# Attention outputs turned in 32x32 blocks by VectorE, four heads stacked, with the projection's weights padded to four chunks of 128

## The chip, the cores and the metric

The kernel runs on one core of a Trainium2 chip. The metric is the device time of one execution in microseconds, given as the median of several runs. Times inside the program come from one profiled execution on the same kind of chip.

## The reference

One transformer block is computed: 2048 tokens, width 448, 16 heads of 28, a causal sliding window of 256 keys, a feed-forward part of width 1792 with Mish. Both halves are modulated by a conditioning vector.

```python
mod = (silu(c) @ w_mod).reshape(1, 6, 1, -1)
sa, ca, ga, sb, cb, gb = mod[:, 0], ..., mod[:, 5]
h = layernorm(x) * (1 + ca) + sa
q, k, v = split(h @ wqkv)                      # 16 heads of 28
p = softmax(mask(q @ k.T * 28 ** -0.5))        # 0 <= query - key < 256
x = x + ga * ((p @ v).concat_heads @ wo)
h = layernorm(x) * (1 + cb) + sb
x = x + gb * (mish(h @ w1 + b1) @ w2)
```

## The kernel before

The tokens are worked off in four groups of 512. Almost every product is made of two or three matmuls on the high and low parts of its operands (names with h and l: `hh`, `hl`, `Ph`, `Pl`, `wo3`, `wol`), so that float32 accuracy is kept.

**Heads.** There are 64 head steps s (4 groups of 16 heads), each of three units u = 3s + k, with k from 0 to 2. `A(i, t)` makes the scores of head i, queries t*128 onward, in a PSUM bank `sA` (two banks), and VectorE reduces them at once to a row maximum (`junk`, `mx`, L680, with an accumulator read). `M2(pr)` lets TensorE transpose the maxima of two heads (L686), VectorE splits them in two rows `mr`, and a DMA puts them beside q, so that `B(u)` computes scores less the maximum in `sB`. ScalarE takes the exponential twice (`P`, `Ph`), GpSimd subtracts to get `Pl` (`SP`, L730), and `PV` multiplies both with v into a bank `pv`: rows 0 to 27 and 28 hold the high part and the sum of weights, rows 32 to 59 the low part. A head's scores are made three heads ahead of their use.

**Outputs.** `EV` (L746; the last three heads on VectorE, L748) copies the 60 rows of `pv` to one of two tiles `O2`, two heads above each other. `E` (L754) lets TensorE transpose such a pair in four pieces into a bank `tr`; `E2` (ScalarE) copies the low part, `E3` takes the reciprocal of the sum, adds, and GpSimd multiplies into `on[g]`, tokens in the partitions. When all 16 heads of a group are there (`on_full`), `gen_oT` turns `on[g]` back with 16 TensorE transposes (`ot`, through `tr_chunk`, L249), ScalarE makes `hho`, VectorE `hlo`, and `gen_wo` multiplies with the output projection: three chunks of 128 features with three matmuls each, and a fourth of 64 with its two halves stacked, 11 matmuls for 128 tokens. Its result is added to x, stored to `x1d`, and its layer norm statistics taken.

**Order.** It is written out by hand: the loop at the end emits, for each unit u, the attention steps, and between them pieces of a filler (`fill_main`: query, key and value products, `gen_oT`, `gen_wo`, then layer norm and `gen_hT` of the next group) as long as a credit of `RATE[g]` lasts; each yield of the filler costs some of it. `fill_side` adds weight preparation, `pipe` delays the steps that empty a bank by a unit or two, and `later` holds DMA issues for the SP queue. Every engine works its own instructions in that order. `gen_hT` transposes the normed x into a bank, ScalarE makes `hh` (L256), VectorE scales the bank in place (`hT_y`, L253) and subtracts (L261).

**PSUM.** Eight banks: two `sA`, two `sB`, two `mm`, one `pv`, one `tr`, of which M2's and E's transposes share the last. After the heads the banks are given to the feed-forward: two `z`, four `acc`, two `tr`.

**Feed-forward.** For each n, 11 matmuls make `z` (L915), ScalarE Mish and `ah`, VectorE `al`, and 12 matmuls go to `acc` (L1098 to L1100). In the first 14 of them the weights are still split (`pieces`: ScalarE, then GpSimd), and a filler works off the projection of group 3, `gen_oT(3)` and `gen_wo(3)`, a few steps for each n.

Of the kernel before, what the change touches and what calls it, by code (L numbers as in the profile page):

```python
# [15 lines left out]
NG, GT = 4, 512  # L16
# [35 lines left out]
def adaln_block(ctx: ExitStack, tc: tile.TileContext, x, wqkv, wo, w1, b1, w2, c, w_mod, out):  # L52
# [104 lines left out]
    mask = kq.tile([128, 384], F32, name="mask")  # L157
# [100 lines left out]
    def hT_lo(p, ci, hh, hl, si, y=True):  # L258
        if y:
            hT_y(p, ci, si)  # L260
        DVE.tensor_tensor(hl[:, ci], p, hh[:, ci].bitcast(F32), op=ALU.subtract)  # L261
# [49 lines left out]
    def tile_mms(p, ps):  # L311
        m = 0
        for n, (a, b) in enumerate(ps):
            PE.matmul(p, b, a, start=(n == 0), stop=(n == 10))  # L314
            m += 1
            if m >= chunk["v"] and n < 10:
                yield cost(m, p.shape[-1])
                m = 0
# [181 lines left out]
    first_tiles([(0, bank("pv", 1, "qk0_0")), (3, bank("tr", 1, "qk0_3"))])  # L500
# [17 lines left out]
    O2 = []  # L518
    for i in range(2):
        t = att.tile([128, GT], F32, name=f"o2_{i}")  # L520
        POOL.memset(t[32:64, :], 0.0)
        O2.append(t)
    wo3 = [mid.tile([128, D], F32R, name=f"wo3_{i}", tag="wo", bufs=7) for i in range(4)]
    wol = [mid.tile([128, D], F32R, name=f"wol_{i}", tag="wo", bufs=7) for i in range(3)]
# [5 lines left out]
    def stg(pl, name):  # L530
        return pl.tile([128, 512], F32, name=name, tag="stg", bufs=4)
# [19 lines left out]
    def gen_mod_wo():  # L551
# [6 lines left out]
        pieces = []  # L558
        for ci in range(4):
            t = stg(qk, f"wop{ci}")  # L560
            pieces.append(t[:, 0:D])
            later.append(lambda ci=ci, t=t: load_piece(wo, ci, 0, D, t))
# [3 lines left out]
        for ci in range(4):  # L566
# [5 lines left out]
            split_lo(w, wo3[ci], wol[min(ci, 2)], ci, DVE)  # L572
# [40 lines left out]
    def gen_oT(g, tag, bufs, oT_pool):  # L613
        o = on[g]
        oh, ol = OT[g] = new_T(f"o{g}", oT_pool)

        def oT_out(p, ci):
            DVE.tensor_tensor(ol[:, ci], p, oh[:, ci].bitcast(F32), op=ALU.subtract)

        for ci in range(4):  # L620
            p = bank(tag, bufs, f"ot{g}{ci}")
            tr_chunk([o[:, t] for t in range(4)], ci, p)
            ACT.activation(oh[:, ci], p, AF.Copy)
# [12 lines left out]
    def gen_wo(g, tag, bufs):  # L636
# [14 lines left out]
        for t in range(4):  # L651
# [7 lines left out]
            for ci in range(3):  # L659
                ps += [(oh[:, ci, ts], wo3[ci]), (oh[:, ci, ts], wol[ci]), (ol[:, ci, ts], wo3[ci])]  # L660
            ps += [(oh[:, 3, ts], wo3[3]), (ol[:, 3, ts], wo3[3])]
# [6 lines left out]
    mx, Pt, Ph, Pl, pvb, et, olt = {}, {}, {}, {}, {}, {}, {}  # L668
    junk = att.tile([128, 384], F32, name="junk")

    def A(i, t):
# [5 lines left out]
        p = bank("sA", 2, f"sA{i}_{t}")  # L677
# [6 lines left out]
    def M2(pr):  # L684
        p = bank("tr", 1, f"mt{pr}")
# [57 lines left out]
    def EV(i):  # L743
        o = O2[i // 2 % 2][64 * (i % 2):64 * (i % 2) + 60]
        if i < NS - 3:
            ACT.activation(o, pvb[i][0:60, :], AF.Copy)  # L746
        else:
            DVE.tensor_copy(o, pvb[i][0:60, :])  # L748

    def E(pr):  # L750
        g, h = divmod(2 * pr, H)
        p = bank("tr", 1, f"et{pr}")
        for t in range(4):
            PE.transpose(p[:, t * 128:t * 128 + 124], O2[pr % 2][0:124, t * 128:(t + 1) * 128], ident[0:124, 0:124])  # L754
        et[pr] = p.rearrange("p (t a d) -> p t a d", t=4, a=2)

    def E2(pr):
        olt[pr] = att.tile([128, 4, 2, 28], F32, name=f"ol{pr}", tag="ol", bufs=2)
        ACT.activation(olt[pr], et[pr][:, :, :, 32:60], AF.Copy)

    def E3(pr):
        g, h = divmod(2 * pr, H)
        e, ol = et[pr], olt[pr]
        if h == 0:
            on[g] = mid.tile([128, 4, 512], F32, name=f"on{g}", tag="on")
        rc = att.tile([128, 4, 2, 1], F32, name=f"rc{pr}", tag="rc", bufs=2)
        DVE.reciprocal(rc, e[:, :, :, 28:29])
        DVE.tensor_tensor(ol, ol, e[:, :, :, 0:28], op=ALU.add)
# [411 lines left out]
```

## Time and profile before

| | |
|---|---|
| median of 3 runs | 717.61 us (717.17 to 718.66) |
| profiled execution, and its span | 719.96 us, 718.2 us |
| granted TensorE clock, mean | 0.99 |
| HBM read, written | 53.45 MB, 29.36 MB |
| attention, groups 1 and 2 | 139 to 241 and 241 to 343 us |
| feed-forward alone | from about 415 us |

In the profile PE is TensorE's matmuls, PEld its weight loads, DVE VectorE, ACT ScalarE, POOL GpSimd, SP the queue that issues the transfers. A row of a group names the source line, engine and operation, the tiles it writes and reads, the shape, the count, then busy us and mean ns, and the idle time just before with what ended it. A row of the timeline is start, duration, engine, line, tiles and count. A row of a table by windows gives for each engine the busy time and instructions, in the order PE, PEld, DVE, ACT, POOL, then the granted clock, the DMA share and GB/s.

### The profile page before, as it was taken

Reading aid. Unit: us, or ns where it says so; the run is one execution under the profiler, and the core shown is the slowest. Engines: PE = TensorE matmul, PEld = TensorE weight load, DVE = VectorE, ACT = ScalarE, POOL = GpSimd, SP = SyncE. Lnnn points to the kernel's source line nnn. Section 1 sums busy time; section 2 is a strip of 40 time slices with the busy share of each in tenths; the row PEclk is TensorE's granted clock in tenths of the full one; section 3 lists DMA queues with packets and bytes.
Section 4 is the critical chain, followed back from the end, with each engine's and each line's share of the span. In section 5 each row is a group of like instructions: output and inputs, shape, how many; then the busy total and the mean of one; then the engine's idle time right before and its main releaser. Section 6 shows DMA issues by size and latency. Waiting matters only on the chain.

```text
span 718.2 us, 12057 instructions
## 1 busy us (share of the span) xinstructions
PE 694.9 (97%) x4049; PEld 597.3 (83%) x4049; DVE 380.0 (53%) x1018; ACT 390.9 (54%) x740; POOL 327.0 (46%) x358
## 2 busy tenths in 40 slices
PE   8999999999999999999999899999999999999996
PEld 8777878788898888898887688888888888888885
DVE  5688657788555878656768642434323232322112
ACT  4538778768766768767868774243224222422221
POOL 6636778676666767666869744422010000000002
PEclk9999999999999999999999899999999999999999
DMA  7865763453761653744672165400200020001001
GB/s 215 257 211 178 251 204 122 148 158 125 212 207 50 203 166 88 230 137 137 216 223 75 52 216 157 116 1 2 102 1 1 4 99 1 0 7 45 0 1 51
DMA packets 48249, 83.86 MB, mean 117 GB/s; under 512 B 6142, under 2 KB 26348, under 8 KB 48188
## 3 DMA queue, kind: packets, MB, share of 16 engines
q1 hardware_dynamic: 47724, 83.10, 37.1%
q8 instruction: 32, 0.52, 0.3%
q14 instruction: 29, 0.24, 0.1%
q10 hardware_dynamic: 464, 0.00, 0.0%
HBM read 53.45 MB, written 29.36 MB: 115 GB/s over the span
## 4 chain that ended last, share of the span: by engine, by line
PE 72%; issue 11%; DVE 8%; DMA 4%; ACT 2%; POOL 1%; SPq 1%; POOLq 0%; DVEq 0%; ACTq 0%
PE z L915 15%; PE pv L740 9%; PE qk L314 8%; PE sA L678 5%; PE acc L1098 5%; PE acc L1100 5%; PE acc L1099 5%; PE sB L708 5%; PE wo L314 4%; PE qk_v L314 4%; PE sB L719 3%; DVE junk L680 3%; PE et L754 2%; DMA q<-mr 1%; DMA scr<-st 1%
## 5 line engine op out<-in xcount | busy, mean ns | idle before, releaser
L730 POOL TENSOR_TENSOR Pl<-P,Ph 128x512 fp32r<-128x512 f32 (+2 forms) x192 | 234.5, 1229 | 87.1 <-ACT Ph L723 49.4
L680 DVE CUSTOM_DVE_ANT_0 junk<-sA,mask 128x384 f32<-128x384 f32 (+2 forms) x256 | 135.2, 528 | 97.8 <-PE sA L678 89.5
L722 ACT ACTIVATE P<-sB 128x512 f32<-128x512 f32 (+2 forms) x192 | 109.8, 572 | 66.9 <-PE sB L719 61.7
L923 DVE TENSOR_TENSOR al<-t,ah 128x512 fp32r<-128x512 f32 x56 | 38.7, 692 | 199.7 <-ACT ah L922 199.7
L921 ACT ACTIVATE t<-z,b1c 128x512 f32<-128x512 f32 x56 | 38.5, 688 | 188.8 <-PE z L915 181.6
L723 ACT ACTIVATE Ph<-sB 128x512 fp32r<-128x512 f32 (+2 forms) x192 | 109.2, 569 | 0.0
L678 PE MATMUL sA<-k,q 84*128 84x384 f32 (+2 forms) x256 | 100.9, 396 | 2.2 <-DVE mx L680 1.5
L915 PE MATMUL z<-hhf,w 128*128 128x512 f32 x224 | 89.6, 400 | 0.0
L915 PE MATMUL z<-hlf,w 128*128 128x512 f32 x224 | 88.4, 395 | 0.0
L1098 PE MATMUL acc<-w2h,ah 128*128 128x448 f32 x224 | 82.0, 366 | 0.0
L1100 PE MATMUL acc<-w2h,al 128*128 128x448 f32 x224 | 81.7, 365 | 0.0
L1099 PE MATMUL acc<-w2l,ah 128*128 128x448 f32 x224 | 81.4, 364 | 0.0
L740 PE MATMUL pv<-Ph,v 128*60 128x256 f32 (+2 forms) x352 | 77.6, 295 | 3.6 <-DVE o L748 2.3
L740 PE MATMUL pv<-Pl,v 128*60 128x256 f32 (+2 forms) x352 | 74.4, 286 | 2.3 <-POOL Pl L730 2.3
L708 PE MATMUL sB<-q,k 86*128 86x256 f32 (+1 forms) x352 | 74.7, 286 | 1.4 <-DMA q<-mr 1.4
L915 PE MATMUL z<-hhf,w1l 128*128 128x512 f32 x168 | 66.3, 395 | 0.0
L708 PEld LDWEIGHTS sB<-q,k 86*128 86x128 f32 x352 | 62.4, 191 | 2.9 <-issue 1.2
L740 PEld LDWEIGHTS pv<-Ph,v 128*60 128x60 f32 x352 | 46.0, 135 | 18.0 <-ACT o L746 3.2
L719 PE MATMUL sB<-fdmask,identr 128*128 128x128 bf16 (+1 forms) x320 | 60.6, 255 | 0.0
L678 PEld LDWEIGHTS sA<-k,q 84*128 84x128 f32 x256 | 48.9, 192 | 8.5 <-DVE mx L680 5.9
L740 PEld LDWEIGHTS pv<-Pl,v 128*60 128x60 f32 x352 | 45.7, 133 | 11.0 <-POOL Pl L730 3.9
L1107 POOL TENSOR_TENSOR yo<-yo,x 128x448 f32<-128x448 f32 (+1 forms) x4 | 4.2, 1064 | 108.1 <-DVE yo L1104 108.1
(156 smaller groups left out, 1300.4 us busy)
## 6 DMA issues: line engine op xcount, KB each, us to landing
scr<-st SPq DMA_DIRECT2D x24, 512.0 KB
k<-scr SPq DMA_DIRECT2D x48, 252.0 KB
q<-scr SPq DMA_DIRECT2D x64, 168.0 KB
scr<-st SPq DMA_DIRECT2D x32, 256.0 KB
x<-x1d SPq DMA_DIRECT2D x10, 448.0 KB
xin<-in_A_x_dram SPq DMA_DIRECT2D x8, 448.0 KB
xr<-in_A_x_dram SPq DMA_DIRECT2D x16, 224.0 KB
x1d<-xr SPq DMA_DIRECT2D x16, 224.0 KB
```

The source lines that it names most:

```text
L314: PE.matmul(p, b, a, start=(n == 0), stop=(n == 10))
L678: PE.matmul(p[:, c0:384], q[0:84, t * 128:(t + 1) * 128], k[0:84, t * 128 + c0:t * 128 + 384], start=True, stop=True)
L680: DVE.tensor_tensor_reduce(out=junk[:, c0:384], in0=p[:, c0:384], in1=mask[:, c0:384], scale=1.0, scalar=-3.0e38, op0=ALU.add, op1=ALU.max ...
L708: PE.matmul(p[:, c:c + 128 * (t1 - t0)], k[:, jj * 128:(jj + 1) * 128], q[:, t0 * 128:t1 * 128], start=(n == 0), stop=False, skip_group_ch ...
L722: ACT.activation(P[:, c0:], p[:, c0:], AF.Exp, scale=SCALE)
L723: ACT.activation(Ph[u][:, c0:], p[:, c0:], AF.Exp, scale=SCALE)
L730: eng.tensor_tensor(Pl[u][:, a:b], Pt[u][:, a:b], Ph[u][:, a:b].bitcast(F32), op=ALU.subtract)
L740: PE.matmul(pv[0:60, t0 * 128:t1 * 128], V[j % NV][:, h, :], P[u][:, c:c + 128 * (t1 - t0)], start=(P is Ph and b == 0 and n == 0), stop=F ...
L915: PE.matmul(zb[n], ps[m][1], ps[m][0], start=(m == 0), stop=(m == 10))
L1098: PE.matmul(p, ah[n][:, ts], w2h[f], start=(f == 0), stop=False)
L1099: PE.matmul(p, ah[n][:, ts], w2l[f], start=False, stop=False)
L1100: PE.matmul(p, al[n][:, ts], w2h[f], start=False, stop=(f == NF - 1))
```

## The change

Head outputs are now kept with the features in the partitions. `EV` copies only the low part, 28 rows, to a place of `OL4` that belongs to the head's place among four; `EA` adds it to the high part on VectorE, into `O4`. After four heads, `T1` turns `O4` in 32x32 blocks on VectorE into `T4`, the reciprocal of the sums is taken, GpSimd multiplies, and a step later `T2` turns `T4` back into chunk `on[g][:, ci]`. So `on[g]` holds four chunks of 4 x 32 rows as the projection needs them; `gen_oT` has only `hho` (ScalarE) and `hlo` (VectorE and GpSimd by turns) to make and yields twice instead of four times (eight times for the last group). The projection's weights are laid out in four chunks of 4 x 32 rows, 28 of them filled, by 16 transfers; it takes 12 matmuls for 128 tokens. The bank `tr` falls away in the attention: `pv` has two banks, and `M2` writes into the unused columns 384 to 512 of the latest `sA` bank. The scaling of `hT` in the attention goes from VectorE to ScalarE. `mask` and `junk` become bf16.

```diff
 def hT_lo(p, ci, hh, hl, si, y=True):
-    if y:
+    if y and si == 0:
+        ACT.activation(p, p, AF.Identity, scale=cols[:, 1, ci:ci + 1], bias=cols[:, 0, ci:ci + 1])
+    elif y:
         hT_y(p, ci, si)
...
+    def wo_load(ci, t):
+        for a in range(4):
+            r = (4 * ci + a) * DH
+            dma(t[32 * a:32 * a + DH], wo[r:r + DH, :])
...
     for ci in range(4):
-        p = bank(tag, bufs, f"ot{g}{ci}")
-        tr_chunk([o[:, t] for t in range(4)], ci, p)
-        ACT.activation(oh[:, ci], p, AF.Copy)
-        pipe.add(1, lambda p=p, ci=ci: oT_out(p, ci))
+        ACT.activation(oh[:, ci], o[:, ci], AF.Copy)
+        (DVE, POOL)[ci % 2].tensor_tensor(ol[:, ci], o[:, ci], oh[:, ci].bitcast(F32), op=ALU.subtract)
         if ci < 3:
             later.append(lambda t=ci: xr_load(g, t))
-        yield
-        if g == NG - 1:
+        if ci % 2:
             yield
...
-    p = bank("sA", 2, f"sA{i}_{t}")
+    p = last["A"] = bank("sA", 2, f"sA{i}_{t}")
...
 def M2(pr):
-    p = bank("tr", 1, f"mt{pr}")
+    p = last["A"][:, 384:512]
     PE.transpose(p[0:8, 0:128], mx[pr].rearrange("p a t -> p (a t)"), ident)
...
-        pvb[i] = bank("pv", 1, f"pv{i}")
+        pvb[i] = bank("pv", 2, f"pv{i}")
...
+def EA(i):
+    a = i % 4 * 32
+    DVE.tensor_tensor(O4[a:a + 32], pvb[i][0:32, :], OL4[a:a + 32], op=ALU.add)
+
+def T1(qd):
+    DVE.transpose(T4, O4)
+    rc = att.tile([128, 16, 1], F32, name=f"rc{qd}", tag="rc", bufs=1)
+    o = T4.rearrange("p (b d) -> p b d", d=32)
+    DVE.reciprocal(rc, o[:, :, 28:29])
+    POOL.tensor_tensor(o[:, :, 0:28], o[:, :, 0:28], rc.to_broadcast([128, 16, 28]), op=ALU.mult)
+
+def T2(qd):
+    g, ci = divmod(qd, 4)
...
+    DVE.transpose(on[g][:, ci], T4)
+    if ci == 3:
         on_full.add(g)
...
+        if k == 0 and 0 <= s - 2 < NS:
+            EA(s - 2)
+        if k == 2 and s % 4 == 1 and s > 4:
+            T1((s - 5) // 4)
+        if k == 2 and s % 4 == 2 and s > 5:
+            T2((s - 6) // 4)
```

The order of TensorE around the maxima's transpose, in the first unit of head step 17 of the kernel before; `mt` is the bank of that transpose, `sA_0` the bank of head 20's first scores, and the brackets name the engines whose progress the row waits for.

```order
L708 MATMUL sB_1966<-q_2_459,k_5_460 128x128
L719 LDWEIGHTS identr
L719 MATMUL sB_1966<-fdmask,identr 128x128
L719 LDWEIGHTS identr
L719 MATMUL sB_1966<-fdmask,identr 128x256
L678 MATMUL sA_0_1978<-k_2_145,q_1_458 128x384 [waits DMAHW6_49,DMAHW5_49,DVE_49]
L686 MATMUL mt_1981<-ident,mx_1804 8x128 [waits DVE_49]
L314 MATMUL qk_6_1988<-hh_754,wq_105 128x512 [waits DVE_49]
L314 MATMUL qk_6_1988<-hh_754,wql 128x512
```

The same place of the changed kernel:

```order
L719 LDWEIGHTS identr
L719 MATMUL sB_1926<-fdmask,identr 128x256
L678 MATMUL sA_0_1938<-k_2_145,q_1_458 128x384 [waits DMAHW1_49,DMAHW0_49,DVE_49]
L686 MATMUL sA_0_1938<-ident,mx_1774 8x128 [waits DVE_49]
L316 MATMUL qk_6_1948<-hh_753,wq_105 128x512
L316 MATMUL qk_6_1948<-hh_753,wql 128x512
```

The row keeps its place, but it now writes the tile of the row ahead of it; the VectorE instruction that it waits for was the last maximum of head 19 and is now the accumulator read of head 20's first reduction, which follows the row ahead.

GpSimd at the seam from the attention to the feed-forward, before (`on` is the attention's output, `w2l`, `w1l` and `w` the split weights of the feed-forward):

```order
L770 TENSOR_TENSOR on_5218<-ol_6147,rc_6168 128x4x56
L770 TENSOR_TENSOR on_5218<-ol_6212,rc_6214 128x4x56
L772 COPY on_5218<-on_5218 128x4x64
L885 TENSOR_TENSOR w2l_6248<-w2p_6137,w2h_6247 128x448
L197 TENSOR_TENSOR w1l<-w1p_6233,w_5270 128x448
L199 TENSOR_TENSOR w_5270<-w1p_6235,w_5270 64x448
L885 TENSOR_TENSOR w2l_6316<-w2p_6238,w2h_6315 128x448
```

And after:

```order
L759 TENSOR_TENSOR t_464<-t_464,rc_5939 128x16x28
L879 TENSOR_TENSOR w2l_5972<-w2p_5840,w2h_5971 128x448
L197 TENSOR_TENSOR w1l<-w1p_5957,w_5049 128x448
L199 TENSOR_TENSOR w_5049<-w1p_5959,w_5049 64x448
L624 TENSOR_TENSOR hlo_6003<-on_5223,hho_6002 128x512 x2
L879 TENSOR_TENSOR w2l_6044<-w2p_5962,w2h_6043 128x448
```

The two `hlo` of chunks 1 and 3, which VectorE made before, stand on GpSimd behind the split of the first three weight pieces.

TensorE at the same seam, before, from the last rows of the first `acc` round on:

```order
L1099 MATMUL acc_3_6265<-w2l_6157,ah_6178 128x448
L1100 MATMUL acc_3_6265<-w2h_6156,al_6179 128x448
L249 MATMUL ot_6280<-ident,on_5218 128x128 x4
L249 MATMUL ot_6289<-ident,on_5218 128x128 x4
L915 MATMUL z_6297<-hhf_5889,w_5270 128x512
L915 MATMUL z_6297<-hhf_5889,w1l 128x512
```

And after:

```order
L1093 MATMUL acc_3_5989<-w2l_5891,ah_5908 128x448
L1094 MATMUL acc_3_5989<-w2h_5890,al_5909 128x448
L316 MATMUL wo_0_6018<-wo_0_466,hho_6002 128x448
L316 MATMUL wo_0_6018<-wol_470,hho_6002 128x448
L316 MATMUL wo_0_6018<-wo_0_466,hlo_6003 128x448
L316 MATMUL wo_0_6018<-wo_1_467,hho_6002 128x448
L316 MATMUL wo_0_6018<-wol_471,hho_6002 128x448
L316 MATMUL wo_0_6018<-wo_1_467,hlo_6003 128x448
L909 MATMUL z_6025<-hhf_5595,w_5049 128x512
```

The first half of the projection's first output tile stands where the first transposes stood, two rounds earlier than before.

More of the change, by code (lines that the diff above doesn't have):

```diff
@@ L313, in tile_mms @@
         for n, (a, b) in enumerate(ps):
-            PE.matmul(p, b, a, start=(n == 0), stop=(n == 10))
+            PE.matmul(p, b, a, start=(n == 0), stop=(n == len(ps) - 1))
             m += 1
-            if m >= chunk["v"] and n < 10:
+            if m >= chunk["v"] and n < len(ps) - 1:
                 yield cost(m, p.shape[-1])
@@ L516, in adaln_block @@
     k3_tile(att, NK - 1)
[L518 to L524, printed above, removed]
+    O4, OL4, T4 = [att.tile([128, GT], F32, name=n) for n in ("o4", "ol4", "t4")]
+    POOL.memset(OL4, 0.0)
+    wo3 = [mid.tile([128, D], F32R, name=f"wo3_{i}", tag="wo", bufs=8) for i in range(4)]
+    wol = [mid.tile([128, D], F32R, name=f"wol_{i}", tag="wo", bufs=8) for i in range(4)]
     def xr_tile(name):
```

64 lines of the change are left out of this document (19 added, 45 removed).

## The prediction

> **What bounds the kernel now.** I read the page's totals first, then the stages, then the waits, then single units in the order of time.
>
> ```profile
> span 718.2 us, 12057 instructions
> PE 694.9 (97%) x4049; PEld 597.3 (83%) x4049; DVE 380.0 (53%) x1018; ACT 390.9 (54%) x740; POOL 327.0 (46%) x358
> ...
> 241.00:292.00 51.00, 49.21 (x341) 42.36 (x340) 40.62 (x119) 37.76 (x73) 37.68 (x37) 1.00 0.52 159
> 292.00:343.00 51.00, 50.91 (x343) 44.56 (x342) 30.62 (x102) 35.22 (x70) 33.42 (x30) 1.00 0.53 161
> ```
>
> One attention group of 16 heads takes 102 us, and TensorE is busy for 50.9 of the 51 us of its second half. In the first half, where the layer norm, the hT chunks and the output projection run beside the heads, TensorE has 1.8 us of holes and VectorE is busy for 40.6 us of 51. After about 415 us only feed-forward matmuls are left. So TensorE's instruction stream is the bound: work taken from it is time won, and a wait put into it is time lost. The waits of TensorE between 43 and 415 us (columns: total us, times, longest us) show how little it waits now:
>
> ```profile
> PE pv L740 <- POOL Pl L730: 2.3, 6, 0.5
> PE pv L740 <- DVE o L748: 2.3, 1, 2.3
> PE tr L249 <- DVE hl L261: 1.6, 2, 0.8
> PE mt L686 <- DVE mx L680: 1.5, 3, 0.7
> PE sA L678 <- DVE mx L680: 1.5, 5, 0.4
> PE sB L708 <- DMA q<-mr: 1.4, 2, 0.7
> PE pv L740 <- ACT o L746: 1.2, 3, 0.6
> ```
>
> **The change part by part.** The profiled execution took 719.96 us (span 718.2); the median of the runs is 717.61, so 2.35 less. I add to 719.96 and subtract 2.35 at the end.
>
> *Transposes that leave TensorE.* Start-to-start distances, not the 0.27 us of one record, are what four of them cost:
>
> ```profile
> 261.24 0.59 PE L754 MATMUL et<-ident,o 124*128 124x124 f32 x4
> 261.58 0.45 PE L314 MATMUL wo<-wol,hho 128*128 128x448 f32 x1
> ...
> 263.55 0.37 PE L314 MATMUL wo<-wo,hlo 128*128 128x448 f32 x1
> 263.76 0.37 PE L314 MATMUL wo<-wo,hho 128*128 128x448 f32 x1
> ...
> L754 PE MATMUL et<-ident,o 124*128 124x124 f32 x128 | 19.3, 273 | 0.0
> L249 PE MATMUL ot<-ident,on 128*128 128x128 f32 x64 | 9.4, 272 | 0.0
> ```
>
> Four take 0.34 us of the stream. 128 et and 64 ot are 48 such fours: 16.3 us leave. The projection gets a twelfth matmul for each of its 16 output tiles (four full chunks of three, where the fourth had two): 16 x 0.21 = 3.4 us come in. Net **-12.9 us** (at 0.11 us each, if nothing around them is hidden: 192 x 0.11 - 3.4 = -17.7).
>
> [...]
>
> *The maxima's transpose (M2).* This is the largest term. Its bank "tr" is gone; it now writes columns 384 to 512 of the sA tile that the matmul just ahead of it has filled, and VectorE is reading that tile. In the built program it waits for that reduction's accumulator read; before, it waited for the pair ahead, mostly done. A quiet unit, a narrow one of group 0 and one with VectorE behind:
>
> ```profile
> 51.64 0.28 PE L686 MATMUL mt<-ident,mx 128*8 128x128 f32 x1
> 52.06 0.08 DVE L680 DVE_READ_ACCUMULATOR2_ANT mx<- 128x1 f32 x1
> ...
> 269.75 0.27 PE L686 MATMUL mt<-ident,mx 128*8 128x128 f32 x1
> 270.74 0.08 DVE L680 DVE_READ_ACCUMULATOR2_ANT mx<- 128x1 f32 x1
> ...
> 293.24 0.27 PE L686 MATMUL mt<-ident,mx 128*8 128x128 f32 x1
> 293.93 0.08 DVE L680 DVE_READ_ACCUMULATOR2_ANT mx<- 128x1 f32 x1
> ```
>
> From the transpose's start to the end of that read are 294.01 - 293.24 = 0.77 us (quiet), 0.50 (narrow) and 1.07 (behind). TensorE works in order, so filler, PV and the next scores stand behind it. The 32 M2 calls less the first and the last, which waited for the newest reduction already, leave 30: 6 narrow, 24 wide. With half of the wide ones behind, 6 x 0.50 + 12 x 0.77 + 12 x 1.07 = 25.1 us; at least 21.5 with all quiet. While TensorE stands, the others catch up: of the waits for Pl, hl and mx above (6.9 us) I take 2.5 back. Net **+22.6 us**. [...]
>
> *Two banks for pv.* The waits for ACT o (1.2 us) go; the wait of 2.3 us for DVE o belongs to the tail below. With the weight loads that stood before them, **-1.5 us**.
>
> *VectorE, ScalarE, GpSimd in the groups.* Nearest rows:
>
> ```profile
> L261 DVE TENSOR_TENSOR hl<-tr,hh 128x512 fp32r<-128x512 f32 x16 | 11.1, 692 | 0.8 <-ACT tr L456 0.4
> L253 DVE TENSOR_SCALAR tr<-tr,cols 128x512 f32<-128x512 f32 x14 | 11.4, 814 | 0.7 <-ACT hh L256 0.7
> L618 DVE TENSOR_TENSOR hlo<-ot,hho 128x512 fp32r<-128x512 f32 x16 | 11.0, 688 | 7.2 <-ACT hho L623 7.2
> L768 DVE TENSOR_TENSOR ol<-ol,et 128x224 f32<-128x224 f32 x32 | 10.7, 335 | 0.0
> L767 DVE RECIPROCAL rc<-et 128x8 f32<-128x8 f32 x32 | 6.5, 202 | 1.6 <-ACT ol L759 1.6
> L730 POOL TENSOR_TENSOR Pl<-P,Ph 128x512 fp32r<-128x512 f32 x155 | 201.4, 1304 | 76.8 <-ACT Ph L723 40.2 <-PE pv L740 9.8 <-PE sA L678 9.4
> L770 POOL TENSOR_TENSOR on<-ol,rc 128x224 f32<-128x224 f32 x32 | 18.0, 564 | 23.5 <-DVE ol L768 11.0 <-ACT Ph L723 10.1 <-PE ot L249 1.5
> L199 DVE TENSOR_TENSOR wq<-wqs,wq 64x512 fp32r<-64x512 f32 x1 | 1.7, 1677 | 0.0
> ```
>
> No row shows the block transpose. Its bounds are 0.34 (L768) and 1.68 us (L199, the dearest 512 columns); I take 0.69, the usual 512 columns. Per group VectorE gains 16 additions (EA) x 0.69 and 8 block transposes x 0.69 and 4 reciprocals of about 0.2, 17.4 us in all, and loses 8 x 0.335, 8 reciprocals, two hlo and four scalings of tr, 2.7 + 1.6 + 1.4 + 3.3 = 9.0. From 71.2 to some 80 us of about 102: hidden, though it lags more in first halves (counted as "behind"). ScalarE gets four scalings and loses eight smaller copies: about even. GpSimd gets two hlo at 1.3 (as Pl, L730) per group and keeps its multiplications (half as many, twice as wide), beside one Pl in every unit of 102/48 = 2.1 us; since hho and hlo now come in two steps instead of four and the wo matmuls follow at once, **+1.5 us** for three groups (0 to 5). The wo weights load in 16 pieces instead of 5, so 11 more issues stand on SP with q, k and mr transfers of group 0 behind them; the mr wait of 1.4 us above shows that some of these are near: **+0.5** (0, or that wait once more).
>
> *The tail of the attention.*
>
> ```profile
> 405.32 0.34 PE L719 MATMUL sB<-fdmask,identr 128*128 128x128 bf16 x2
> 407.95 0.68 PE L740 MATMUL pv<-Ph,v 128*60 128x128 f32 x2 [2.29 <-DVE o L748]
> ...
> 407.50:414.20 6.70, 6.25 (x31) 5.66 (x32) 2.94 (x6) 3.36 (x8) 2.90 (x3) 0.50 0.00 1
> ```
>
> With one pv bank TensorE waited 2.29 us for a copy stuck in VectorE's queue, and then ran 6.7 us at a granted clock of 0.50, some 3.3 us lost. With two banks it goes on; next late are Pl and the exponentials, nearly as late. Of 5.6 us I take **-3.5**.
>
> *The seam to the feed-forward.* The last group's projection no longer has eight steps of transposes ahead of it: its first six matmuls stand right behind the first twelve acc matmuls.
>
> ```profile
> 420.93 0.45 PE L1098 MATMUL acc<-w2h,ah 128*128 128x448 f32 x1
> 422.03 0.69 DVE L923 TENSOR_TENSOR al<-t,ah 128x512 fp32r<-128x512 f32 x1 [1.62 <-ACT ah L922]
> 423.24 0.34 PEld L249 LDWEIGHTS ot<-ident,on 128*128 128x128 f32 x2
> 424.15 1.16 POOL L885 TENSOR_TENSOR w2l<-w2p,w2h 128x448 fp32r<-128x448 f32 x1
> 425.28 1.14 POOL L197 TENSOR_TENSOR w1l<-w1p,w 128x448 fp32r<-128x448 f32 x1
> 426.50 1.16 POOL L199 TENSOR_TENSOR w<-w1p,w 64x448 fp32r<-64x448 f32 x1
> ```
>
> Measured from the first acc matmul (less 0.4 for the et transposes ahead of it), TensorE is done with acc at +2.5. VectorE ends al at +2.2 and then turns the last four heads: block transpose to +2.9, reciprocal +3.1, GpSimd's product (448 wide, 1.15) +4.3, second transpose +5.0, hlo of chunk 0 at +5.7. GpSimd goes from that product to w2l, w1l, w and only then to hlo of chunk 1: 4.3 + 3.5 + 1.3 = +9.1. The six matmuls need hho0, hlo0, hho1, hlo1 in that order and last 1.2 us, so TensorE stands some 9.1 - 2.5 - 1.0 = 5.6 us, and perhaps at half the clock behind it, as in the tail. I take **+5.5** (0 if GpSimd is early, 9 with the clock).
>
> Sum: -12.9 + 22.6 - 1.5 + 1.5 + 0.5 - 3.5 + 5.5 = +12.2; 719.96 + 12.2 - 2.35 = **729.8 us**.
>
> **The rivals.**
>
> *A, faster.* The transpose waits are mostly paid back: other waits vanish under them, and the seam finds GpSimd early. For: both queues have slack in the second halves (30.6 and 33.4 us of 51). Against: TensorE has hardly any other wait to give back there, and an order on one queue stays an order. Price: the floor of 21.5 less all seven waits' 11.8 less the tail's 2.3 already counted, so 21.5 - 9.5 = 12.0; with -17.7, -1.5, -5.6 and no seam, -12.8, about 705; half way from there to no change, 711. It decides once a wait costs less than some (12.9 + 1.5 + 3.5)/30 = 0.6 us net and the seam nothing. Chance 0.15.
>
> *B, VectorE takes over.* At 1.68 us the 32 block transposes cost 32 more us, 8 per group, and first halves reach some 47 of 51 us; each M2 then waits for a queue that is behind. If half of that shows, +16: about 745. For: two-input rows stretch beside GpSimd. Against: this one has a single input. Chance 0.12.
>
> *C, the clock.* If the M2 waits with VectorE behind make the granted clock fall as the 2.29 us did, each costs half of a 6.7 us stretch: with three or four of them, +12, about 742. Against: single holes of 0.6 to 0.8 us left it at 1.00. [...] Chance 0.07.
>
> That the transposes stay on TensorE after all I exclude: the built program has no L754 left.
>
> **How the numbers follow.** Forecast (0.66): 720 to 738, most likely 729.8. Rivals 0.15, 0.12 and 0.07 at 711, 745 and 742. The range 712 to 742 leaves out half of A and most of B. A measurement of this kernel can tell 0.2%, 1.4 us. Faster: A and little else, 0.16; same, the edge between the forecast and A: 0.05; slower 0.79.
>
> **What would show it.** In the changed kernel's waits, a row of TensorE "sA L686 <- DVE mx" of 30 times and over 15 us, with M2 starting after the accumulator read; no pv wait for a copy near 405; a wait of wo for hlo of 3 to 6 us after the first acc matmuls; VectorE near 80 us in a group. The forecast is wrong if that L686 row is under 8 us, or if a group's period falls under 100 us.

## The result, and the profile after

The changed kernel takes 767.84 us (median of four runs, 766.92 to 768.48) where the kernel before took 717.39 us beside it: ratio 1.0702, interval 1.0679 to 1.0724, or 50.4 us slower. The forecast was 729.8 us, in a range of 712 to 742. The direction was right; the size was not.

The page of the changed kernel opens with the span and the busy times:

```profile
span 765.5 us, 11798 instructions
PE 695.6 (91%) x3873; PEld 586.4 (77%) x3873; DVE 432.8 (57%) x1044; ACT 396.8 (52%) x722; POOL 334.7 (44%) x349
```

TensorE issues 176 matmuls fewer and is busy for 0.7 us longer, in a span 47.3 us longer. So time was lost in two ways: in holes, and in matmuls that run longer. The next rows give the second and third group of heads as one stretch each, first of the kernel before, then of the changed one (window, length, then busy time of TensorE, its weight loads, VectorE, ScalarE, GpSimd, then the granted clock):

```profile
121.50:223.00 101.50, 99.50 (x677) 86.44 (x676) 71.19 (x217) 72.47 (x141) 68.73 (x63) 1.00 0.54 163
223.00:324.90 101.90, 99.85 (x679) 86.66 (x678) 71.02 (x215) 72.15 (x140) 68.64 (x63) 1.00 0.50 154
```

```profile
132.10:243.50 111.40, 97.90 (x633) 83.23 (x632) 83.84 (x221) 73.87 (x136) 70.11 (x60) 0.98 0.48 148
243.50:356.20 112.70, 99.41 (x636) 84.23 (x635) 85.09 (x221) 73.96 (x136) 70.40 (x61) 0.97 0.45 135
```

A group grows by 10 to 11 us. VectorE gains 13 to 14 us of work in it and is still only 75% busy; the clock is no longer 1.00. The waits of TensorE in the changed kernel (total us, times, longest us):

```profile
PE sA L686 <- DVE mx L680: 27.9, 32, 1.9
PE pv L740 <- POOL Pl L730: 9.8, 10, 2.5
PE sA L678 <- DVE mx L680: 9.6, 14, 1.4
PE wo L316 <- POOL hlo L624: 2.4, 1, 2.4
PE wo L316 <- ACT hho L623: 1.7, 1, 1.7
PE wo L316 <- DVE hlo L624: 0.9, 1, 0.9
```

The first row is the forecast one (over 15 us, about 30 times). The second was 2.3 us before and the third 1.5; the last three are the seam. One of the longer M2 waits, TensorE first and then VectorE:

```profile
195.77 0.42 PE L678 MATMUL sA<-k,q 84*128 84x384 f32 x1
197.80 0.27 PE L686 MATMUL sA<-ident,mx 128*8 128x128 f32 x1 [1.61 <-DVE mx L680]
```

```profile
196.58 0.69 DVE L263 TENSOR_TENSOR hl<-tr,hh 128x512 fp32r<-128x512 f32 x1 [1.45 <-ACT tr L260]
197.19 0.55 DVE L680 CUSTOM_DVE_ANT_0 junk<-sA,mask 128x384 bf16<-128x384 f32 x1
197.66 0.08 DVE L680 DVE_READ_ACCUMULATOR2_ANT mx<- 128x1 f32 x1
```

VectorE was not busy: it stood 1.45 us for ScalarE's scaling of tr, with the reduction that M2 needs queued behind hl. So one queue's wait becomes another's.

The clock: rows of windows of the changed kernel, a stretch ahead of a fall and then the falls (last columns: granted clock, DMA share, GB/s).

```profile
260.90:264.30 3.40, 2.04 (x12) 1.16 (x11) 3.08 (x9) 2.85 (x6) 2.99 (x4) 1.00 0.90 310
```

```profile
264.30:271.10 6.80, 5.71 (x22) 4.84 (x23) 6.16 (x11) 3.93 (x8) 6.80 (x6) 0.51 0.24 74
...
424.80:435.00 10.20, 7.15 (x30) 5.82 (x31) 9.44 (x19) 4.29 (x8) 7.80 (x9) 0.50 0.00 1
465.70:475.90 10.20, 7.54 (x18) 5.70 (x19) 1.77 (x2) 0.69 (x2) 5.17 (x4) 0.51 0.49 158
sum 37.40, PE 30.41 PEld 24.96 DVE 23.93 ACT 13.92 POOL 29.20; mean PE 5.07 PEld 4.16 DVE 3.99 ACT 2.32 POOL 4.87
```

Between 45 us and the end of the seam the changed kernel runs 37.4 us at half the clock, the kernel before 6.8. The 30.6 us more are worth 15.3 us of full clock. They are no item of their own in the account further down: they stand behind holes, and are counted with what made these.

The trace's own records of the clock put the six falls at 69.87, 155.21, 264.43, 387.31, 424.86 and 465.82 us. Their distances are 25, 32, 36, 11 and 12 times 3.413 us, so in this execution the falls lie on a fixed grid. In the grid's windows just ahead of a fall TensorE was busy for 0.92 to 2.13 us; five other windows at full clock had 1.81 to 1.99 us, and no fall came behind them. So busy time alone does not part these windows. The longest M2 wait, 1.89 us ahead of 377.80, stands across a border of the grid (377.07), and the clock stayed at 1.00; whether that is why was not tried.

The seam, on TensorE, VectorE and GpSimd:

```profile
464.36 0.47 PE L316 MATMUL wo<-wo,hho 128*128 128x448 f32 x1 [1.70 <-ACT hho L623]
...
465.98 0.74 PE L316 MATMUL wo<-wo,hlo 128*128 128x448 f32 x1 [0.95 <-DVE hlo L624]
...
469.85 0.74 PE L316 MATMUL wo<-wo,hlo 128*128 128x448 f32 x1 [2.38 <-POOL hlo L624]
```

```profile
464.29 0.71 DVE L765 STREAM_TRANSPOSE on<-t 128x512 f32<-128x512 f32 x1 [1.05 <-POOL t L759]
```

```profile
463.32 0.94 POOL L759 TENSOR_TENSOR t<-t,rc 128x448 f32<-128x448 f32 x1 [7.83 <-DVE rc L758]
464.22 1.15 POOL L879 TENSOR_TENSOR w2l<-w2p,w2h 128x448 fp32r<-128x448 f32 x1
465.32 1.59 POOL L197 TENSOR_TENSOR w1l<-w1p,w 128x448 fp32r<-128x448 f32 x1
467.00 1.46 POOL L199 TENSOR_TENSOR w<-w1p,w 64x448 fp32r<-64x448 f32 x1
468.53 2.49 POOL L624 TENSOR_TENSOR hlo<-on,hho 128x512 fp32r<-128x512 f32 x2
```

The order is the one worked out in the prediction: product, w2l, w1l, w, and only then hlo of chunk 1. The wo matmul that needs it, at 469.85, starts 9.8 us behind the first acc matmul, at 460.05.

The added operations, in groups (count, busy us, mean ns):

```profile
L752 DVE TENSOR_TENSOR o<-pv,ol 32x512 f32<-32x512 f32 x64 | 43.5, 679 | 1.5
L759 POOL TENSOR_TENSOR t<-t,rc 128x448 f32<-128x448 f32 x16 | 15.4, 961 | 31.8 <-DVE rc L758 29.1 <-PE sB L719 2.7
L624 POOL TENSOR_TENSOR hlo<-on,hho 128x512 fp32r<-128x512 f32 x8 | 12.0, 1507 | 1.5 <-ACT hho L623 1.4
L765 DVE STREAM_TRANSPOSE on<-t 128x512 f32<-128x512 f32 x16 | 11.3, 706 | 1.1 <-POOL t L759 1.1
L755 DVE STREAM_TRANSPOSE t<-o 128x512 f32<-128x512 f32 x16 | 11.3, 706 | 0.0
L624 DVE TENSOR_TENSOR hlo<-on,hho 128x512 fp32r<-128x512 f32 x8 | 10.1, 1269 | 1.3 <-ACT hho L623 1.1
```

The block transpose takes 0.71 us and the addition 0.68, as assumed (0.69). The low parts are dearer: 1.27 us on VectorE, where the kernel before took 0.69 from PSUM, and 1.51 on GpSimd (1.3 assumed).

### The profile page after: what moved, and what is told of

Read it like the earlier page. It is cut to its first block, busy times and chain, and to the rows that moved or that the text cites. A ratio compares the mean times of both kernels' runs of the same rounds, so it can differ in the third digit from the quotient of the medians.

```text
span 765.5 us, 11798 instructions
## 1 busy us (share of the span) xinstructions
PE 695.6 (91%) x3873; PEld 586.4 (77%) x3873; DVE 432.8 (57%) x1044; ACT 396.8 (52%) x722; POOL 334.7 (44%) x349
## 4 chain that ended last, share of the span: by engine, by line
PE 60%; issue 14%; DVE 10%; ACT 4%; DMA 3%; POOL 3%; SPq 0%; POOLq 0%; DVEq 0%; ACTq 0%
PE z L909 14%; PE pv L740 7%; PE qk L316 6%; PE acc L1094 4%; PE acc L1092 4%; PE acc L1093 4%; PE sA L678 4%; PE wo L316 4%; DVE junk L680 4%; PE sB L708 4%; PE qk_v L316 3%; PE sB L719 3%; DMA scr<-st 1%; POOL Pl L730 1%; ACT Ph L723 1%
## 5 line engine op out<-in xcount | busy, mean ns | idle before, releaser
L730 POOL TENSOR_TENSOR Pl<-P,Ph 128x512 fp32r<-128x512 f32 (+2 forms) x192 | 231.8, 1216 | 111.0 <-ACT Ph L723 68.1
L680 DVE CUSTOM_DVE_ANT_0 junk<-sA,mask 128x384 bf16<-128x384 f32 (+2 forms) x256 | 134.8, 527 | 67.8 <-PE sA L678 55.5
L678 PE MATMUL sA<-k,q 84*128 84x384 f32 (+2 forms) x256 | 103.5, 406 | 10.4 <-DVE mx L680 9.6
L740 PE MATMUL pv<-Pl,v 128*60 128x256 f32 (+2 forms) x352 | 76.0, 290 | 10.1 <-POOL Pl L730 9.8
L678 PEld LDWEIGHTS sA<-k,q 84*128 84x128 f32 x256 | 50.6, 198 | 18.9 <-DVE mx L680 15.4
L746 ACT ACTIVATE ol<-pv 28x512 f32<-28x512 f32 x61 | 35.8, 588 | 34.9 <-PE pv L740 34.0
```

Of the source, the lines that this page charges most:

```text
L678: PE.matmul(p[:, c0:384], q[0:84, t * 128:(t + 1) * 128], k[0:84, t * 128 + c0:t * 128 + 384], start=True, stop=True)
L680: DVE.tensor_tensor_reduce(out=junk[:, c0:384], in0=p[:, c0:384], in1=mask[:, c0:384], scale=1.0, scalar=-3.0e38, op0=ALU.add, op1=ALU.max ...
L730: eng.tensor_tensor(Pl[u][:, a:b], Pt[u][:, a:b], Ph[u][:, a:b].bitcast(F32), op=ALU.subtract)
L740: PE.matmul(pv[0:60, t0 * 128:t1 * 128], V[j % NV][:, h, :], P[u][:, c:c + 128 * (t1 - t0)], start=(P is Ph and b == 0 and n == 0), stop=F ...
```

## The experiments

Times are compared with runs of the kernel before on the same chip, 717.5 to 718.3 us; "above before" is the difference of the two medians. The changed kernel is 50.4 us above before.

**The M2 wait, taken away from the changed kernel.**

```
+        if k == 0 and (a - 1) % 2 == 1 and LEAD <= a - 1 < NS:
+            M2((a - 1) // 2)
         if a < NS:
             A(a, (0, 1, 3)[k])
-        if k == 0 and (a - 1) % 2 == 1 and LEAD <= a - 1 < NS:
-            M2((a - 1) // 2)
```

> The changed kernel with one call moved: the maxima's transpose is issued before the scores A(a, 0) of its unit, so it writes into the tile of the scores of one unit earlier, whose reduction it needs anyway; bank sharing stays. Theory W (the wait and what follows from it is most of the loss): the row sA L686 <- DVE mx falls from 27.9 us to under 5, sA L678 <- DVE mx from 9.6 to under 4, the half-clock stretches inside the attention groups (20 us of them, 10 lost) mostly go; left are the seam and the end of the attention: 712 to 726 us. Rival V (the added work of VectorE and GpSimd slows the stream by itself): only the 27.9 us go, 738 us or more, and the waits for Pl and mx stay.

742.94 us, ratio 1.0341 (1.0306 to 1.0375), 24.7 above before. Its waits:

```profile
PE sA L678 <- DVE mx L680: 13.7, 17, 2.2
PE pv L740 <- POOL Pl L730: 9.8, 12, 2.0
PE wo L316 <- POOL hlo L624: 3.0, 1, 3.0
...
PE sA L686 <- DVE mx L680: 1.5, 3, 0.9
```

The M2 row falls from 27.9 to 1.5 us and the time by 25.8 us (50.4 - 24.7), about the wait itself. Two other things moved with it, one each way: the stretches at half the clock shrank from 37.4 to 20.5 us, worth 8.5 us, and the wait for the scores' banks grew from 9.6 to 13.7. The wait for Pl stayed. Theory W falls here: the other half of the loss does not come from M2. In the second and third group of heads little of the loss is left, 2 us each (net of what the change saves there):

```profile
127.40:231.00 103.60, 97.67 (x633) 83.86 (x632) 83.69 (x221) 73.05 (x135) 70.09 (x60) 0.98 0.50 157
231.00:334.80 103.80, 96.84 (x635) 82.80 (x634) 83.62 (x221) 73.48 (x136) 70.44 (x61) 1.00 0.48 147
```

**The M2 wait, alone, in the kernel before.**

```
-        p = bank("sA", 2, f"sA{i}_{t}")
+        p = last["A"] = bank("sA", 2, f"sA{i}_{t}")
...
-        p = bank("tr", 1, f"mt{pr}")
+        p = last["A"][:, 384:512]
```

> The kernel before with one edit: the maxima's transpose writes into columns 384 to 512 of the scores tile just filled; the four-head transposes stay on TensorE and pv keeps one bank. Theory W: the wait of 22 to 28 us plus 8 to 20 us of half clock and of waits behind it: 748 to 765 us, with at least two half-clock stretches between 45 and 400 us. Rival V: the wait alone, 739 to 745 us, and no half-clock stretch there.

742.61 us, 1.0334 (1.0305 to 1.0363), 24.3 above before. The lines of this kernel are two further down:

```profile
PE sA L688 <- DVE mx L682: 24.3, 32, 1.5
```

The wait is 24.3 us and so is the loss. Between 45 and 400 us one stretch of 3.4 us ran at half the clock, where W asked for two and V for none; over the whole attention it was 10.2 us against 6.8, worth 1.7. Both ways round the price of M2 is 24 to 26 us.

**TensorE working through the M2 wait.**

```
+            for _ in range(6):
+                PE.matmul(pvb[s - 1][0:60, 0:256], zer[:, 0:60], fdmask, start=False, stop=False,
+                          skip_group_check=True)
             M2((a - 1) // 2)
```

> The changed kernel with six matmuls of zero weights (128 x 60, 256 columns, added to the open pv sums) between the scores A(a, 0) and the maxima's transpose: TensorE works through the wait where it stood. Theory C (the waits make the granted clock fall): the row sA L686 <- DVE mx falls below 12 us, the stretches of clock 0.50 at 70, 155, 264 and 387 us (17 us, 8.5 lost) go, and the time is 754 to 763 us although TensorE has 30 x 0.7 us more to do. Rival (the clock falls for the thinner stream as a whole, or for other holes): the stretches stay and the time is 766 us or more.

767.68 us, 1.0682 (1.0650 to 1.0714): no change. The M2 row fell to 5.9 us, as expected, but the row sA <- DVE mx rose from 9.6 to 12.5. The half-clock stretches between 45 and 400 us shrank from 17.0 us (four) to 6.8 (two), and in all from 37.4 to 27.2, worth 5.1 us. Six zero matmuls took 0.77 us at the median; 31 times that is 24 us. Waits down by 22.0 - 2.9 - 0.6 (Pl) = 18.5, clock by 5.1, work up by 24: the sum is near zero, as measured. So M2's waits do take part in the falls of the clock, for some 5 us here; the expected net gain was too high because filling costs as much as waiting.

**The price of the transposes.**

```
-        for t in range(4):
+        for t in (0, 1, 2, 3) * 2:
             PE.transpose(p[:, t * 128:t * 128 + 124], O2...
...
-            tr_chunk([o[:, t] for t in range(4)], ci, p)
+            for _ in range(2):
+                tr_chunk([o[:, t] for t in range(4)], ci, p)
```

> The kernel before with each of its 128 et and 64 ot transposes issued twice (same result). If four cost 0.34 us of the stream, as the distances between starts say: +16 us, 734 us. If each costs its record of 0.27 us: +52 us, 769 us. If they hide beside weight loads: under +5 us.

732.09 us, 1.0186 (1.0154 to 1.0218), 13.8 above before: 192 transposes at 0.072 us each, four in 0.29 us. The distances between starts (0.34) are the right measure, the records (0.27 each) are not.

With theory W gone, the next four runs start from the kernel with the early M2, 24.7 above before.

**The seam.**

```
             if ci % 2:
-                yield
+                for _ in range(4 if g == NG - 1 else 1):
+                    yield
```

> The kernel with the early maxima's transpose (742.9 us, 24.7 above before), and in the last group each pair of hho/hlo chunks is followed by four steps of the filler instead of one, so that the projection's matmuls come behind more feed-forward matmuls. If the seam costs what its rows say (waits of wo for hho, hlo and hlo of 1.4, 1.2 and 3.0 us and half a clock over 6.8 us): 734 to 737 us, and no wait of wo over 1 us. If the late chunks only move the wait: 740 us or more.

735.42 us, 1.0240 (1.0223 to 1.0258): 17.6 above before, 7.1 less. No wait of wo over 1 us is left. The wait did not move elsewhere: the seam cost 7.1 us, somewhat less than its rows (1.4, 1.2 and 3.0 us) with 6.8 us at half the clock behind them.

**One chunk at a time in all groups.**

```
-            if ci % 2:
+            yield
+            if g == NG - 1:
                 yield
```

> As the kernel with the early maxima's transpose, but in every group one filler step behind each of the four chunks (two in the last group), as the kernel before has them. If two chunks at once crowd VectorE and GpSimd: 2 to 5 us below the run that only mends the seam. If the crowding comes from the additions, block transposes and products, which stay: the same as that run within 1.5 us.

735.96 us, 1.0243 (1.0222 to 1.0264): the same as the run before it. That two chunks come at once costs nothing that these runs can tell.

**VectorE's added work out.**

```
+    POOL.memset(T4, 1.0)
...
-        DVE.transpose(T4, O4)
...
-        if k == 0 and 0 <= s - 2 < NS:
-            EA(s - 2)
```

> The kernel with the early maxima's transpose, with VectorE's added work left out: the 64 additions of the attention sums (0.68 us each) and the first of the two block transposes of each four heads (0.71 us each), 54 us in all; the attention outputs are ones in this run. Theory Q (VectorE's bursts hold the scores' banks and so TensorE): the wait sA <- DVE mx falls from 13.7 to under 5 us, and with it half-clock stretches: 722 to 732 us. Rival G (GpSimd is what is late) or order of the stream: 737 us or more.

729.32 us, 1.0160 (1.0122 to 1.0199): 11.5 above before, 13.2 less. Its four runs spread from 726.6 to 732.4, so this is sure to some 3 us. The row sA <- DVE mx went from 13.7 to 9.5 us only:

```profile
PE sA L679 <- DVE mx L681: 9.5, 12, 2.7
PE pv L741 <- POOL Pl L731: 8.2, 10, 2.2
```

So theory Q holds for the time, and its wait row fell less than expected; the holes it names are a part of what the crowding costs.

**GpSimd's added work out.**

```
-            (DVE, POOL)[ci % 2].tensor_tensor(ol[:, ci], o[:, ci], oh[:, ci].bitcast(F32), op=ALU.subtract)
+            if ci % 2 == 0:
+                DVE.tensor_tensor(ol[:, ci], o[:, ci], oh[:, ci].bitcast(F32), op=ALU.subtract)
...
-                ps += [(oh[:, ci, ts], wo3[ci]), (oh[:, ci, ts], wol[ci]), (ol[:, ci, ts], wo3[ci])]
+                ps += [(oh[:, ci, ts], wo3[ci]), (oh[:, ci, ts], wol[ci]), (ol[:, ci // 2 * 2, ts], wo3[ci])]
...
-        POOL.tensor_tensor(o[:, :, 0:28], o[:, :, 0:28], rc.to_broadcast([128, 16, 28]), op=ALU.mult)
```

> The kernel with the early maxima's transpose, with GpSimd's added work left out: the products with the reciprocals (0.96 us each) and the low parts of chunks 1 and 3 (1.65 us each; the matmuls read those of chunks 0 and 2 instead). Theory G (GpSimd's bursts make the low parts of the exponentials late): the wait pv <- POOL Pl falls from 9.8 to under 4 us, the wait of wo for POOL goes: 728 to 734 us. If VectorE alone crowds: 738 us or more, less the seam's 3 us.

732.62 us, 1.0211 (1.0181 to 1.0240): 14.8 above before, 9.9 less. The wait for Pl falls under 4 us and the wait of wo for POOL goes, as theory G has it, while the wait for the scores' banks grows from 13.7 to 18.0:

```profile
PE sA L679 <- DVE mx L681: 18.0, 20, 2.2
...
PE pv L741 <- POOL Pl L731: 2.4, 3, 0.9
```

Q and G were not rivals after all: each engine has its share. How GpSimd's share comes about is seen in the kernel with the early M2. GpSimd:

```profile
142.64 0.94 POOL L759 TENSOR_TENSOR t<-t,rc 128x448 f32<-128x448 f32 x1 [1.36 <-PE sB L719]
143.54 1.28 POOL L730 TENSOR_TENSOR Pl<-P,Ph 128x512 fp32r<-128x512 f32 x1
```

and TensorE:

```profile
144.87 0.45 PE L740 MATMUL pv<-Pl,v 128*60 128x128 f32 x2 [0.42 <-POOL Pl L730]
```

The exponentials of this Pl were ready at 142.19 (ScalarE's `Ph`, 141.60 and 0.59 us long). But GpSimd stood idle until it could begin the product, and the Pl behind it began at 143.54; so TensorE waits 0.42 us for it although GpSimd is busy for two thirds of a group only. In the changed kernel GpSimd stands 29.1 us in all for VectorE's reciprocal in front of its products, where before it stood 11.0 for VectorE's `ol`.

Both runs take out more than the change put in. The kernel before had products and additions of its own: its GpSimd works 327.0 us and its VectorE 380.0, against 334.7 and 432.8 in the changed kernel, and 309.2 (GpSimd, this run) and 373.7 (VectorE, the run before). So 13.2 and 9.9 us are what the new way's work costs against none at all, not against the old way's.

**All three together.** The three diffs shown under "The seam", "VectorE's added work out" and "GpSimd's added work out", in one kernel.

> The three edits that helped the kernel with the early maxima's transpose, together: the last group's projection spread over more steps (-7.5), VectorE's additions and first block transposes left out (-13.6), GpSimd's products and low parts left out (-10.3, of which some 3 are the seam's); the outputs are not those of the computation. If the costs are separate and add: 714 to 717 us. If VectorE and GpSimd delay each other, so that either removal already gave part of the other: 718 us or more. If the transposes and banks saved are to show once the crowding is gone (the prediction's 702 to 706 us): below 710.

716.82 us, 0.9992 (0.9968 to 1.0015): level with before. Single gains were 7.1 + 13.2 + 9.9 = 30.2; together they are 25.8, the seam being in two of them. The costs nearly add. But level with before, with less work on VectorE and GpSimd than before (369.5 and 312.4 us), is not the gain that the saved transposes should give.

**Scaling of tr back on VectorE**, in the kernel with early M2 and mended seam (17.6 above before):

```
-        if y and si == 0:
-            ACT.activation(p, p, AF.Identity, scale=cols[:, 1, ci:ci + 1], bias=cols[:, 0, ci:ci + 1])
-        elif y:
+        if y:
             hT_y(p, ci, si)
```

> The kernel with the early maxima's transpose and the spread projection (735.4 us), with the scaling of tr back on VectorE instead of ScalarE: 4 x 0.81 us a group more on VectorE. If VectorE's queue is what costs: 2 to 4 us slower. If the wait of VectorE for ScalarE's scaling (hl <- ACT tr, 10 us in all) was a cost of its own: as much faster.

737.62 us, 1.0277 (1.0252 to 1.0302), 2.1 more. The intervals just meet, so that the scaling is better off VectorE in the crowded kernel is likely, not sure.

**Scaling of tr on ScalarE, alone, in the kernel before** (the same lines the other way).

> The kernel before with one part of the change: ScalarE scales tr in place of VectorE. The prediction counted this as even: 717 to 719 us. If VectorE then stands behind ScalarE's queue and the scores' reductions behind it: 720 to 724 us.

721.26 us, 1.0041 (1.0026 to 1.0056), 3.3 above before. There VectorE has room, and a wait for ScalarE's longer queue, with reductions behind it, is worse than the work was: VectorE stands 14.6 us in 14 waits for that scaling, and the row sA <- DVE mx goes from 1.5 to 4.3 us.

**The product on VectorE**, in the kernel with early M2 and mended seam:

```
-        POOL.tensor_tensor(o[:, :, 0:28], o[:, :, 0:28], rc.to_broadcast([128, 16, 28]), op=ALU.mult)
+        DVE.tensor_tensor(o[:, :, 0:28], o[:, :, 0:28], rc.to_broadcast([128, 16, 28]), op=ALU.mult)
```

> The kernel with the early maxima's transpose and the spread projection (735.4 us), with the product by the reciprocals on VectorE instead of GpSimd: GpSimd is rid of 15 x 0.96 us ahead of low parts of exponentials, VectorE gets them. If GpSimd's place ahead of Pl costs more than the same on VectorE: 728 to 733 us. If VectorE's queue is the dearer: 737 us or more.

739.38 us, 1.0295 (1.0275 to 1.0316), 3.8 more than with the product on GpSimd. The Pl row fell from 8.6 to 3.2 us and the row sA <- DVE mx rose from 12.4 to 19.2: the load moves, and VectorE is the dearer place.

**Where the saving went.** The kernel with all three edits, with the scaling of tr put back (as above):

> The run with the three edits together (716.8 us; the last group's projection spread, VectorE's additions and first block transposes, GpSimd's products and low parts left out), with the scaling of tr back on VectorE. If ScalarE's scaling costs 3.3 us here as alone in the kernel before: 712 to 715 us. If it costs nothing here (as in the crowded kernel, where putting it back gave 2.2 us more): 716 us or more.

714.40 us, 0.9966 (0.9941 to 0.9992): 3.1 below before. Its interval meets that of the run with all three edits, so the 1.9 us between them are not sure.

And besides without the rest of the turning:

```
-            ACT.activation(oh[:, ci], o[:, ci], AF.Copy)
-            if ci % 2 == 0:
-                DVE.tensor_tensor(ol[:, ci], o[:, ci], oh[:, ci].bitcast(F32), op=ALU.subtract)
+            ACT.activation(oh[:, ci], ident[:, 0:1].to_broadcast([128, GT]), AF.Copy)
...
-        rc = att.tile([128, 16, 1], F32, name=f"rc{qd}", tag="rc", bufs=1)
-        o = T4.rearrange("p (b d) -> p b d", d=32)
-        DVE.reciprocal(rc, o[:, :, 28:29])
...
-        DVE.transpose(on[g][:, ci], T4)
```

> The same, and besides without the second block transposes, the reciprocals and VectorE's low parts (16 x 0.71, 16 x 0.25, 8 x 1.26 us); the projection reads ones. Nothing of the turning of the attention outputs is left on VectorE and GpSimd; TensorE is without the 192 transposes (13.8 us) and has the 16 matmuls (3.4). If the saving is real: 702 to 708 us. If the transposes were mostly hidden in this stream: 712 us or more.

710.91 us, 0.9909 (0.9889 to 0.9928): 6.6 below before, between the two expectations. The saving is real, and about half of what it should be (how much of it is the transposes' is asked further down). Where some of the rest goes shows in this kernel: the scores' row is still 7.6 us (7 times, longest 2.1), against 1.5 before. At the longest of these holes VectorE stood, and SyncE had just issued loads of xr:

```profile
250.28 0.62 DVE L637 TENSOR_TENSOR xr<-xr,wo 128x448 f32<-128x448 f32 x1 [2.54 <-PE sB L717]
```

```profile
245.25 2.65 SPq L59 DMA_DIRECT2D xr<-in_A_x_dram  x3
```

The addition of the projection to xr seems to wait for its load, since the projection now comes sooner: it starts 5.0 us behind the issue of that load, where in the kernel before the same addition started 12.7 us behind it and VectorE did not stand. That is read from the times of rows and was not tried.

**Additions or block transposes.** The kernel with the early M2, without the additions alone:

```
-        if k == 0 and 0 <= s - 2 < NS:
-            EA(s - 2)
```

> The kernel with the early maxima's transpose (742.9 us) without the 64 additions (43.5 us of VectorE); both block transposes stay. Additions and first block transposes together were 13.6 us. If the cost goes by VectorE's time: 4/5 of it, 731 to 733 us. If the block transposes, which come in one piece with a reciprocal behind them, weigh more than their time: 735 us or more.

731.69 us, 1.0189 (1.0169 to 1.0208): 14.2 above before, 10.5 less. Of VectorE's 13.2 us the 64 additions have 10.5 (43.5 us of work), and 2.7 are left for the 16 first block transposes (11.3 us); the intervals of the two runs meet, so the 2.7 are not sure. The additions cost a quarter of a microsecond for each microsecond of VectorE, and the block transposes fit that. Those that the change is named for are the smaller part.

## Why the prediction was wrong

The account of the 50.4 us, each item from a pair of runs: M2 +25.8; seam and the bulk of the added work of VectorE and GpSimd, together, +25.8; ScalarE's scaling +1.9 (unsure); second block transposes, reciprocals and VectorE's low parts +3.5; what is left, the saving, -6.6. They add up by construction, being one chain of kernels. By place, in one profiled execution of each (us from the start to the first M2, on to the last M2, on to the end of the last PV, and on to the end; M2 by the starts of its rows on TensorE):

| kernel | to first M2 | heads | tail | rest |
|---|---|---|---|---|
| before | 43.4 | 355.5 | 19.1 | 300.1 |
| changed | 45.1 | 397.7 | 14.8 | 307.9 |
| early M2 | 44.8 | 372.8 | 14.8 | 306.8 |
| all three edits | 45.2 | 355.4 | 14.5 | 298.5 |
| and without the rest of the turning | 44.3 | 351.1 | 14.6 | 298.5 |

The prediction's steps in turn:

*Transposes that leave TensorE, -12.9.* Doubling them gave 13.8, where 16.3 was taken; with the 3.4 for the twelfth matmuls, which was not measured alone, -10.4. The reading by distances between starts held, with 0.072 us each by the doubled run. The 0.11 us behind the other bound, -17.7, is shown by no run. In the rearranged kernel 6.6 us came out, with the two banks for pv and the tail in it. Of the 9.8 us between the profiled executions the tail has 4.5 and the heads only 4.4 (355.5 - 351.1), so this term came short as well. The longer waits for the scores' banks in that kernel, 7.6 against 1.5 us, are of the size of what is missing; that they are its cause was not tried.

*M2, +22.6.* Right in place and size: 27.9 us in 32 waits (25.1 in 30 forecast), 24.3 to 25.8 us of time. The term was 3.2 us short, mostly because the relief of 2.5 us did not come; the waits for Pl and mx grew from 3.8 to 19.4 us.

*Two banks for pv, -1.5, and the tail, -3.5.* The waits for copies of pv are gone, as forecast. The gain of the tail came, in the stretch from the last M2 to the last PV:

```profile
398.93:418.04 19.11, 16.19 (x102) 14.13 (x103) 11.67 (x22) 14.69 (x28) 11.52 (x12) 0.82 0.19 57
```

```profile
442.88:457.65 14.77, 12.76 (x90) 10.36 (x91) 13.20 (x23) 13.30 (x25) 10.07 (x11) 1.00 0.25 70
```

That is 4.3 us, a part of it the transposes that are gone there. The kernels with one pv bank take 16.9 to 19.1 us for this stretch, those with two 14.5 to 15.9. What went wrong lies ahead of it: in the heads of the last group Pl and the scores' reductions were late, and 10.2 us from 424.8 ran at half the clock. That "next late are Pl and the exponentials, nearly as late" was the right worry, but it struck a few heads earlier.

*VectorE, ScalarE and GpSimd in the groups, +1.5.* This is the step that failed. It added busy times ("From 71.2 to some 80 us of about 102: hidden"), and these were nearly right: 84 to 85 us. But hidden does not follow. With the seam taken off, the work left out cost some 18.7 us (25.8 - 7.1), and the scaling, the second transposes and the low parts up to 5.4 more: 24.1 against 1.5. The table has 17.4 us of it between the first and the last M2 (372.8 - 355.4); by groups that is 4.3, 3.4, 1.9 and 7.8. The last group alone lost more than the upper bound of 5 that the term had for three groups. All this is the price of the new way's work against none; what the old way's work cost was not measured. VectorE works its queue in order and the scores have two banks: with the early M2, where VectorE is busy for 81% of the second and third group, TensorE stood 17 times, 13.7 us in all, for a reduction that came later than these banks cover. The bound "0 to 5" came from the same argument, so the range shared its fault.

*wo loads, +0.5.* Not tried alone. The row sB <- DMA q<-mr did not grow (1.1 us, 1.4 before).

*Seam, +5.5.* Right in mechanism, order and rows; 7.1 us with the clock behind it.

Of the 38.2 us between the forecast's +12.2 and the measured +50.4, 22.6 belong to the work of VectorE, ScalarE and GpSimd, 11.3 to the saving (transposes, banks and tail, -17.9 forecast, -6.6 left), 3.2 to M2 and 1.6 to the seam, less the 0.5 of the loads.

*Rival A* needed waits that pay each other back; they added instead. *Rival B* asked for a block transpose of 1.68 us; it takes 0.71. Single rows of the kernel before show two-input rows both ways: `wol`, 128x448 on VectorE, took 0.62 us at 103.92 with no row of GpSimd beside it and 1.03 us at 109.12 beside GpSimd's Pl, but `w1l` of the same shape took 0.62 us at 367.52 beside Pl too. What B describes, reductions late in VectorE's queue, came at the cheap price too, so it was no matter of that price. *Rival C* had its mechanism, with 15.3 us lost at half the clock where 12 were said, but M2's waits have only a part of that: 8.5 us went when M2 was moved, 5.1 when its waits were filled, and alone in the kernel before it brought 1.7. Against C stood that single holes of 0.6 to 0.8 us left the clock alone. But in the 3.4 us ahead of 264.3, behind which the clock fell, TensorE was busy for 2.04 and no hole was over 0.9, and a single hole of 1.89 us left it alone. The stretches at half the clock lasted 3.4, 6.8 and 10.2 us, one to three steps of the grid, and no window ahead of one was idle: TensorE worked for 0.92 to 2.13 us in each. What decides which windows fall was not shown.

The forecast stayed on the right side because M2 alone outweighs the saving. No version of the changed kernel with the whole computation beat the kernel before; the best, with early M2 and mended seam, is 17.6 us above it. Open are the remaining 9 us of the saving (10.4 for the transposes by the doubled run, 15.4 with pv banks and tail, against 6.6), what the old way's own work on VectorE and GpSimd cost, and the twelfth matmuls and the loads by themselves.

## What to carry to other kernels

Where one in-order engine feeds a saturated one through two buffers, price added work on it by what it stands ahead of, not by whether its total fits; here each microsecond of additions on VectorE cost about a quarter. A write into a buffer that another engine is reading cost here what was left of that read, 0.8 to 0.9 us at each of 32 calls, and moving the call ahead of the next write instead of behind it gave 25.8 us back. Sum the holes over some 3.4 us before calling any of them too small for the clock: here TensorE was busy for 0.92 to 2.13 of the 3.41 us ahead of each fall, and ahead of one of them no hole was over 0.9 us.

## What was not expected of the hardware

The clock fell to half behind windows in which TensorE worked for up to 2.13 of 3.41 us by the records, and the six falls of the changed kernel's profiled execution lie on a grid of 3.413 us. The subtraction of two SBUF inputs took VectorE 1.27 us for 128x512 in the mean, against 0.69 with one input in PSUM. Its single rows took from 0.69 us, at 156.97, to 1.71, at 268.91, both beside rows of GpSimd. It was still 1.17 us with the products and GpSimd's low parts taken out, when GpSimd had the Pl to do. In the feed-forward `al`, of the same shape and from two SBUF inputs too, took 0.69 us in the mean of 56, beside GpSimd for 0.18 us at most. No run tried the subtraction with GpSimd idle, so its cause is not shown. Filling a wait with harmless matmuls took 10.2 of 37.4 us at half the clock away and won nothing.
